# One 4 MB K tile per batch in a cached-attention decode kernel: five shared buffers of 32 KB, all V products by two chunks

## The chip, the cores and the metric

The kernel runs on one core of a Trainium2 chip. The metric is the device time of one execution in microseconds (us). Inputs lie in HBM and are read once.

## The reference

One token for each of eight batches is decoded: layer norm, attention over the last 2048 positions of a cache with 32 query heads that share 8 key heads, an output projection, and a gate from a small MLP.

```python
B, Sq, D = 8, 1, 512
Hq, Hkv, Sk, Dh = 32, 8, 8192, 128
W = min(4096, max(256, Sk // 4))                 # 2048
xn = layernorm(x)
q = (xn @ wq).reshape(B, Sq, Hq, Dh)             # -> b h q d
k = repeat(k_cache[:, :, Sk - W:, :], 4, axis=1) # v alike
p = softmax(einsum("bhqd,bhkd->bhqk", q, k) * Dh ** -0.5)
s = einsum("bhqk,bhkd->bhqd", p, v) -> reshape(B, Sq, Hq * Dh) @ wo
h = sigmoid(xn @ w_gate) * (xn @ w_up)           # D x F, F = 1792
g = silu(h @ w_down)
return x + s * g
```

All tensors are bf16. K and V of the window are 33.6 MB each, wq and wo 4.2 MB each, the three MLP weights 1.8 MB each: 81 MB in all.

## The kernel before

**Loads.** Everything big goes through one ring of nine buffers of 16 KB per partition (2 MB each). A tile of K or V is half a batch: four heads (a "group" gg), 2048 keys; partition p*4+j holds 64 consecutive keys of head j, one run of 16 KB. wq is two tiles, the MLP weights one each, wo two. `loads` lists them by their due times: K tile i at slot 4i, V tile i at slot 4i + 15 (`PV_LAG`), with wg and wu ahead of the last two V tiles, and wd and wo at the end. All are issued by SP, in that order, by `issue_loads()`: load n waits until load n - 9 has been used.

**Slots.** The main loop runs over 64 + 15 slots t, 8 slots per batch; the order in which it writes instructions is the order on each engine. In slot t:

- `k_turn(t)` (L422, DVE): a quarter of K tile t // 4 is transposed in place in 32x32 blocks of 4 byte words, one instruction of 128x1024.
- `qk(t - 4)` (L435, PE): four score matmuls side by side, one for each head of the group, on one of four classes j of the feature index. The moving operand is K with a step of eight elements (16 bytes); it runs over all 512 (chunk, key) columns of the tile. Eight slots fill one PSUM tile `s_ps` for all 32 heads of a batch.
- the softmax of the batch whose scores are complete, spread over phases: maximum `mx` (L447) and `mj` behind the turn in phase 0, `mb` on PE and the exponential on ACT in phase 1, a turn of the probabilities (`pt_bf`, L475) and 16 spreading matmuls (L486) in phase 2, a mask per head on DVE (L506) in phase 3, the denominators (`den_ps`, L528, L530) in phase 4.
- `pv(t - 15)` (L549, PE): a quarter of a V tile against the probabilities. The first six V tiles (`PV_WIDE`) take four chunks of 128 features per matmul (512 columns, weights 64 wide), the others two (256 columns, weights 32 wide). After four slots ACT copies the result, and `pv_sum` (L570, L577) folds the chunks and divides.

So the softmax of batch b - 1 and its V products run among the turns and scores of batch b. The buffers of `mb`, `den_ps`, `oT_ps`, `o2_ps` and `b_ps` are one PSUM bank in turn ("misc").

**The end.** After slot u = 55 of `pv`, `unit_in` multiplies wg and wu (L316), `unit_mid` makes the hidden vector (L330 to L334), `o_rows` (L592, L601) lays the attention output out as rows, `unit_out` multiplies wd (L342), and 64 matmuls with wo (L662) follow as its parts land; `prod` and `y_bf` (L673, L675) and two stores close the kernel.

Of the kernel before, what the change touches and what calls it, by code (L numbers as in the profile page):

```python
# [10 lines left out]
def kernel(  # L11
# [21 lines left out]
    KT = D // P  # L33
# [23 lines left out]
    NA = Dh // 64  # L57
    C4 = 4
    CB = CH // C4
    PV_WIDE = 6  # L60
    RING = 9
    NCOL = 2
    DC = D // NCOL

# [25 lines left out]
            q = nc.sync  # L90
        q.dma_start(out=dst, in_=src)

    def ring_tile(shape, name):
        return ring.tile(shape, bf16, name=name, tag="ring", align_bytes=ALIGN)

    x_bf = work.tile([B, D], bf16, name="x_bf")
    nc.scalar.dma_start(out=x_bf[:], in_=A_x.flatten_outer_dims())

    wq_view = A_wq.rearrange("(p kt) n -> p kt n", kt=KT)
    KH = KT // 2  # L100
    wq_sb = []
    for kh in range(2):
        t = ring_tile([P, KH, Hq * Dh], f"wq_sb{kh}")
        load(t[:], wq_view[:, kh * KH : (kh + 1) * KH, :])
        wq_sb.append(t)

    k_tiles = {}
    v_tiles = {}

    def load_kv(cache, i, name):  # L110
        b, gg = divmod(i, NG)
        t = ring_tile([P, CH, Dh], name)
        load(
            t[:].rearrange("p c d -> p (c d)"),
            cache[b, GL * gg : GL * (gg + 1), win0:Sk, :].rearrange(
                "j (p c) d -> p j (c d)", c=CH
            ),
        )
        return t

    wg_sb = []
    wu_sb = []
    wd_sb = []

    def load_mlp(kind):
        if kind == 2:
            t = ring_tile([P, FT, D], "wd_sb")
            load(t[:], B_w_down.rearrange("(p t) n -> p t n", t=FT))
            wd_sb.append(t)
        else:  # L130
            t = ring_tile([P, KT, F], ("wg_sb", "wu_sb")[kind])
            load(t[:], (B_w_gate, B_w_up)[kind].rearrange("(p kt) n -> p kt n", kt=KT))
            (wg_sb, wu_sb)[kind].append(t)

    loads = [
        (kind, i)
        for _, kind, i in sorted(  # L140
            [(NJ * i, 0, i) for i in range(NT)]
            + [(NJ * i + PV_LAG, 1, i) for i in range(NT)]
        )
    ]
    loads[-2:-2] = [(2, 0), (2, 1)]
    loads = [(4, 0), (4, 1)] + loads + [(2, 2), (3, 0), (3, 1)]
    loads_done = [2]
    released = set()
    wo_view = A_wo.rearrange("(hg p j) n -> p hg j n", p=P, j=4)
    wo_parts = {}  # L150

    def load_wo(half):
        t = ring_tile([P, HG // 2, 4, D], f"wo_sb{half}")
        for h0, h1, j0, j1 in (
            ((0, 2, 0, 4), (2, 4, 0, 4)),
            ((4, 5, 0, 4), (5, 6, 0, 4), (6, 7, 0, 4), (7, 8, 0, 2), (7, 8, 2, 3), (7, 8, 3, 4)),
        )[half]:
            o = half * (HG // 2)
            load(t[:, h0 - o : h1 - o, j0:j1, :], wo_view[:, h0:h1, j0:j1, :])
            for hg in range(h0, h1):  # L160
                for j in range(j0, j1):
                    wo_parts[hg, j] = t[:, hg - o, j, :]

    def issue_loads():
        while loads_done[0] < len(loads):
            n = loads_done[0]
            if n >= RING and loads[n - RING] not in released:
                break
            kind, i = loads[n]
            if kind == 0:  # L170
                k_tiles[i] = load_kv(A_k_cache, i, "k_sb")
            elif kind == 1:
                v_tiles[i] = load_kv(A_v_cache, i, "v_sb")
            elif kind == 2:
                load_mlp(i)
            else:
                load_wo(i)
            loads_done[0] += 1

    issue_loads()  # L180
# [102 lines left out]
    )  # L283

    Sel = {}
    for w in (32, 64):
        Sel[w] = consts.tile([P, w], f32, name=f"Sel{w}")
        nc.vector.tensor_reduce(
            out=Sel[w][:],
            in_=ident[:].rearrange("p (a m) -> p m a", m=w),  # L290
            axis=AX.X,
            op=ALU.add,
        )
# [44 lines left out]
    def unit_out():  # L338
        b_ps = psum1.tile([NCOL * 32, DC], f32, name="b_ps", tag="misc")
        for t in range(FT):  # L340
            for j in range(NCOL):
                nc.tensor.matmul(  # L342
                    b_ps[32 * j : 32 * (j + 1), :],
                    lhsT=hT_sb[:, t, :],
                    rhs=wd_sb[0][:, t, DC * j : DC * (j + 1)],
                    start=(t == 0),
                    stop=(t == FT - 1),
                    tile_position=(0, 32 * j),
                    skip_group_check=True,
                )  # L350
        sigb = work.tile([NCOL * 32, DC], f32, name="sigb")
        nc.scalar.activation(out=sigb[:], in_=b_ps[:], func=AF.Sigmoid)
        nc.vector.tensor_tensor(out=gate[:], in0=sigb[:], in1=b_ps[:], op=ALU.mult)

# [43 lines left out]

    q_tiles = q_projection()
    q_out(0, q_tiles[0], (0, 1))  # L400
    released |= {(4, 0), (4, 1)}
    issue_loads()

    s_tiles = {}
# [8 lines left out]

    def k_turn(t):

        i, j = divmod(t, NJ)
        kw = (
            k_tiles[i][:, CC * j : CC * (j + 1), :]
            .rearrange("p c d -> p (c d)")
            .bitcast(f32)  # L420
        )
        nc.vector.transpose(out=kw, in_=kw)  # L422

    def qk(t):

        i, j = divmod(t, NJ)
        b, gg = divmod(i, NG)
        a, e = divmod(j, 2)
        if gg == 0 and j == 0:
            s_tiles[b] = psum.tile([P, CH * KQ], f32, name="s_ps")  # L430
        kT = k_tiles[i][:].rearrange(
            "p c (a k g e) -> p c a k g e", a=NA, k=KQ, e=2
        )
        for gl in range(GL):
            nc.tensor.matmul(  # L435
                s_tiles[b][32 * gl : 32 * (gl + 1), :],
                lhsT=qz_sb[:, b, GL * gg + gl, j, :],
                rhs=kT[:, :, a, :, gl, e],
                start=(gg == 0 and j == 0),
                stop=(gg == NG - 1 and j == NJ - 1),  # L440
                tile_position=(0, 32 * gl),
                skip_group_check=True,
            )
# [10 lines left out]
    def soft_exp(b, mj):  # L454
        mb_ps = psum1.tile([P, NQ], f32, name="mb_ps", tag="misc")
        nc.tensor.matmul(mb_ps[:], lhsT=SumM[:], rhs=mj[:], start=True, stop=True)  # L456
        nm = small.tile([P, 1], f32, name="nm")
        nc.vector.tensor_reduce(out=nm[:], in_=mb_ps[:], axis=AX.X, op=ALU.min)  # L458
        den128 = small.tile([P, 1], f32, name="den128")
        p_bf = ppool.tile([P, CH * KQ], bf16, name="p_bf")  # L460
        nc.scalar.activation(  # L461
            out=p_bf[:],
            in_=s_tiles.pop(b)[:],
            func=AF.Exp,
            bias=nm[:],
            scale=scale,
            accum_out=den128[:],
        )
        e_tiles[b] = (p_bf, den128)
# [65 lines left out]
    def pv(t):  # L535
# [1 line left out]

        i, j = divmod(t, NJ)
        b, gg = divmod(i, NG)
        n_ch = 4 if i < PV_WIDE else 2  # L540
        w = 16 * n_ch
        if j == 0:
            acc_tiles[i] = psum.tile([P, n_ch * Dh], f32, name="acc_ps")
# [66 lines left out]
    for t in range(NSLOT + PV_LAG):  # L610
# [47 lines left out]
    a_ps = psum.tile([NCOL * 32, DC], f32, name="a_ps", tag="wide")
# [52 lines left out]
```

## Time and profile before

| | |
|---|---|
| time, median of 3 runs (lowest, highest) | 198.31 us (198.0, 199.24) |
| the profiled execution: time, span | 198.21 us, 196.5 us |
| PE busy, DVE busy, ACT busy | 138.2, 117.0, 32.6 us |
| main DMA queue | 81.01 MB, 97.1% of 16 engines' span |
| K turns, L422 | 64 of 1219 ns |
| score matmuls, L435 | 256 of 1065 ns, four at a time |
| V products, L549 | 416 of 345 ns, overlapping |

The span is the time from the first to the last recorded instruction; the execution's own time is 1.71 us longer. Busy times count a stretch once in which instructions overlap, so four matmuls of 1065 ns side by side are about one such stretch. The clock column of the windows is the share of TensorE's full clock that was granted.

### The profile page before, as it was taken

What the parts mean: (1) busy time and instruction counts of PE and PEld (TensorE: products, weight loads), DVE (VectorE), ACT (ScalarE), POOL (GpSimd) and SP (SyncE); (2) the same over time, 40 slices, a digit from 0 to 9 for tenths busy, and PEclk for the clock granted to TensorE, in tenths of its full rate; (3) what the DMA queues carried; (4) which work ended last, traced back from release to release, by engine and by line L of the source; (5) the groups of instructions that cost most, each with busy time, mean ns of one, the idle gap of its engine ahead of it and who ended that gap; (6) DMA issues with size and microseconds to landing.
All of it is one profiled execution on the core that took longest, in us unless ns stands there. A gap on an engine that the chain in (4) does not pass through costs nothing.

```text
span 196.5 us, 2699 instructions
## 1 busy us (share of the span) xinstructions
PE 138.2 (70%) x1112; PEld 57.6 (29%) x1112; DVE 117.0 (60%) x200; ACT 32.6 (17%) x68; POOL 9.3 (5%) x21
## 2 busy tenths in 40 slices
PE   0340078669998987899789278946794779674783
PEld 0110011032324222423333044404240424443661
DVE  3818999746686828664777277837773750361101
ACT  3008540410121102101210021002100210340000
POOL 8820000000000000000000000000000000000000
PEclk9999999955999997879999957996888587996579
DMA  6999999999999999999999999999999999999991
GB/s 215 429 427 427 430 434 429 440 434 427 434 427 434 427 427 427 430 434 430 430 434 434 424 427 440 430 425 427 430 434 430 427 431 434 423 424 420 411 391 41
DMA packets 6860, 81.19 MB, mean 413 GB/s; under 512 B 792, under 2 KB 1088, under 8 KB 2112
## 3 DMA queue, kind: packets, MB, share of 16 engines
q1 hardware_dynamic: 6752, 81.01, 97.1%
q8 instruction: 8, 0.13, 0.2%
q10 hardware_dynamic: 32, 0.01, 0.1%
q14 instruction: 4, 0.03, 0.0%
q0 software_dynamic: 64, 0.01, 0.0%
HBM read 81.02 MB, written 0.01 MB: 412 GB/s over the span
## 4 chain that ended last, share of the span: by engine, by line
DMA 72%; DVE 17%; PE 8%; ACT 1%; issue 1%; SPq 0%; DVEq 0%; ACTq 0%
DMA k_sb<-in_A_k_cache_dram 47%; DMA wd_sb<-in_B_w_down_dram 14%; DVE k_sb L422 11%; DMA wq_sb<-in_A_wq_dram 6%; DMA wo_sb<-in_A_wo_dram 5%; PE pT_ps L486 3%; PE s_ps L435 3%; DVE qz_sb L395 2%; PE acc_ps L549 1%; DVE mx L447 1%; DVE qT_sb L386 1%; DVE pt_bf L475 1%; ACT L461 1%; PE q_ps L367 1%; PE mb_ps L456 0%
## 5 line engine op out<-in xcount | busy, mean ns | idle before, releaser
L422 DVE STREAM_TRANSPOSE k_sb<-k_sb 128x1024 f32<-128x1024 f32 x64 | 75.9, 1219 | 16.6 <-DMA k_sb<-in_A_k_cache_dram 16.5
L435 PE MATMUL s_ps<-k_sb,qz_sb 128*32 128x512 bf16 x256 | 68.7, 1065 | 16.4 <-DVE k_sb L422 11.6
L549 PE MATMUL acc_ps<-v_sb,pT_sb 128*32 128x256 bf16 (+1 forms) x416 | 35.3, 345 | 3.9 <-DMA v_sb<-in_A_v_cache_dram 2.6
L549 PEld LDWEIGHTS <-pT_sb 128*32 128x32 bf16 (+1 forms) x416 | 12.5, 109 | 33.2 <-issue 27.0
L506 DVE TENSOR_SCALAR pT_sb<-pc_bf,Hm 128x512 bf16<-128x512 bf16 x32 | 9.1, 349 | 18.3 <-ACT pc_bf L495 18.3
L435 PEld LDWEIGHTS <-qz_sb 128*32 128x32 bf16 x256 | 8.3, 100 | 34.0 <-issue 26.1
L560 ACT COPY acc_sb<-acc_ps 128x256 f32<-128x256 f32 (+1 forms) x16 | 7.2, 453 | 63.2 <-PE acc_ps L549 63.2
L486 PE MATMUL pT_ps<-pt_bf,spread 128*128 128x128 bf16 x128 | 12.5, 272 | 6.3 <-DVE pt_bf L475 6.3
L570 PEld LDWEIGHTS oT_ps<-Sel,acc_sb 128*128 128x128 f32 x88 | 11.8, 202 | 14.3 <-ACT acc_sb L560 8.5
L570 PE MATMUL oT_ps<-Sel,acc_sb 128*128 128x16 f32 x88 | 13.4, 276 | 1.1 <-ACT acc_sb L560 1.1
L486 PEld LDWEIGHTS <-spread 128*128 128x128 bf16 x128 | 10.8, 123 | 10.8 <-DVE pt_bf L475 10.8
L456 PE MATMUL mb_ps<-mj,SumM 128*128 128x4 f32 x16 | 3.5, 286 | 14.3 <-DVE mj L449 14.3
L461 ACT ACTIVATE p_bf<-s_ps,nm 128x512 bf16<-128x512 f32 x8 | 5.5, 687 | 46.5 <-DVE nm L458 46.5
L577 DVE TENSOR_TENSOR oT_sb<-oT_ps,rden 128x16 bf16<-128x16 f32 x16 | 2.6, 160 | 11.7 <-PE oT_ps L570 11.7
L456 PEld LDWEIGHTS mb_ps<-mj,SumM 128*128 128x128 f32 x16 | 2.8, 218 | 22.5 <-DVE mj L449 20.6
L397 ACT COPY qz_sb<-qT_sb 32x128 bf16<-32x128 bf16 x20 | 8.3, 413 | 3.0 <-DVE qT_sb L386 2.7
L530 DVE RECIPROCAL rden<-den_ps 128x32 f32<-128x32 f32 x8 | 2.8, 351 | 7.3 <-PE den_ps L528 7.3
L495 ACT CAST pc_bf<-pT_ps 128x512 bf16<-128x512 f32 x8 | 4.7, 587 | 13.1 <-PE pT_ps L486 13.1
L367 PE MATMUL q_ps<-wq_sb,xnT_sb 128*32 128x512 bf16 x32 | 3.8, 625 | 4.0 <-DMA wq_sb<-in_A_wq_dram 4.0
L475 DVE STREAM_TRANSPOSE pt_bf<-p_bf 128x512 bf16<-128x512 bf16 x8 | 5.4, 679 | 1.9 <-ACT p_bf L461 1.9
L662 PE MATMUL a_ps<-wo_sb,o_sb 128*32 128x256 bf16 x64 | 5.5, 315 | 1.0 <-DMA wo_sb<-in_A_wo_dram 0.9
L447 DVE TENSOR_REDUCE mx<-s_ps 128x1 f32<-128x512 f32 x8 | 5.3, 657 | 0.0
(61 smaller groups left out, 61.9 us busy)
## 6 DMA issues: line engine op xcount, KB each, us to landing
k_sb<-in_A_k_cache_dram SPq DMA_DIRECT2D x16, 2048.0 KB, 31.8
v_sb<-in_A_v_cache_dram SPq DMA_DIRECT2D x16, 2048.0 KB, 29.5
wq_sb<-in_A_wq_dram SPq DMA_DIRECT2D x2, 2048.0 KB, 9.7
wo_sb<-in_A_wo_dram SPq DMA_DIRECT2D x2, 1024.0 KB
wg_sb<-in_B_w_gate_dram SPq DMA_DIRECT2D x1, 1792.0 KB, 29.3
wu_sb<-in_B_w_up_dram SPq DMA_DIRECT2D x1, 1792.0 KB, 30.1
wd_sb<-in_B_w_down_dram SPq DMA_DIRECT2D x1, 1792.0 KB, 27.6
wo_sb<-in_A_wo_dram SPq DMA_DIRECT2D x3, 512.0 KB, 23.5
```

Of the source, the lines that this page charges most:

```text
L397: nc.scalar.copy(out=out, in_=in_)
L422: nc.vector.transpose(out=kw, in_=kw)
L435: nc.tensor.matmul(s_tiles[b][32 * gl : 32 * (gl + 1), :], lhsT=qz_sb[:, b, GL * gg + gl, j, :], rhs=kT[:, :, a, :, gl, e], start=(gg == 0 ...
L447: nc.vector.reduce_max(out=mx[:], in_=s_tiles[b][:], axis=AX.X)
L456: nc.tensor.matmul(mb_ps[:], lhsT=SumM[:], rhs=mj[:], start=True, stop=True)
L461: nc.scalar.activation(out=p_bf[:], in_=s_tiles.pop(b)[:], func=AF.Exp, bias=nm[:], scale=scale, accum_out=den128[:],)
L475: nc.vector.transpose(out=pt_bf[:].rearrange("p c g q r -> p (c g q r)"), in_=p_bf[:])
L486: nc.tensor.matmul(pT_ps[:, :, c4, :], lhsT=spread[:, c4, Q, :], rhs=pt[:, :, Q, :], start=(Q == 0), stop=(Q == NQ - 1), skip_group_check= ...
L506: nc.vector.tensor_scalar(out=pT_tiles[b][:, :, gl, :], in0=pc, scalar1=Hm[:, gl : gl + 1], scalar2=None, op0=ALU.mult,)
L549: nc.tensor.matmul(acc_tiles[i][w * c : w * (c + 1), :], lhsT=pT[:, 32 * y : 32 * y + w], rhs=v_tiles[i][:, ch : ch + n_ch, :].rearrange(" ...
L560: nc.scalar.copy(out=acc_sb[:], in_=acc_tiles.pop(i)[:])
L570: nc.tensor.matmul(oT_ps[:], lhsT=acc_sb[:, Dh * c : Dh * (c + 1)], rhs=sel[:, c // 2, c % 2], start=(c == 0), stop=(c == n_ch - 1),)
```

## The change

K comes as one tile of 4 MB for each batch: all eight heads, partition p*8+h holds 128 consecutive keys of head h, one run of 32 KB. Each buffer of the ring is 32 KB per partition, and there are five. V of a batch is one buffer too, filled by two loads of 2 MB as before; wq is one buffer with two loads, wg and wu share one, wd and wo have one each. The order of the loads is written out: wq, K0, then K(i+1) and V(i) in turn, V7, wg and wu, wd, wo. So the MLP's input weights now come behind the last V.

The turns of a batch (eight instructions of the same size) are written in the first four of its eight slots, two in each. A score matmul takes one head's feature class over all 128 chunks of the tile, with a step of sixteen elements (32 bytes). The four heads of a matmul group are half of the tile's heads, and the first slot's group already reads the whole length of every partition. The exponential writes its output in the old order of keys. K of a batch is released at the end of slot 11 counted from its own first, V at the end of its eight slots.

All V products take two chunks. `unit_in` for wg is written after slot u = 59 and for wu after u = 63, and `unit_mid` follows there.

```diff
-    PV_WIDE = 6
-    RING = 9
+    RING = 5
+    PK = P // Hkv
+    CK = W // PK
+    KK = PK // NQ
+    HS = CK // CH
+    KS = 2
+    CT = CK // (SPB)
...
-    def ring_tile(shape, name):
-        return ring.tile(shape, bf16, name=name, tag="ring", align_bytes=ALIGN)
+    def ring_tile(name):
+        return ring.tile([P, UNIT], bf16, name=name, tag="ring", align_bytes=ALIGN)
...
+    def load_k(b):
+        t = ring_tile("k_sb")
+        load(
+            t[:],
+            A_k_cache[b, :, win0:Sk, :].rearrange("h (p c) d -> p h (c d)", c=CK),
+        )
+        k_tiles[b] = t[:].rearrange("p (c d) -> p c d", d=Dh)
+
+    def load_v(b):
+        t = ring_tile("v_sb")
+        for gg in range(NG):
+            h = t[:, HALF * gg : HALF * (gg + 1)]
+            load(
+                h,
+                A_v_cache[b, GL * gg : GL * (gg + 1), win0:Sk, :].rearrange(
+                    "j (p c) d -> p j (c d)", c=CH
+                ),
+            )
+            v_tiles[NG * b + gg] = h.rearrange("p (c d) -> p c d", d=Dh)
...
+    loads = [(5, 0), (0, 0)]
+    for i in range(B - 1):
+        loads += [(0, i + 1), (1, i)]
+    loads += [(1, B - 1), (2, 0), (3, 0), (4, 0)]
+    loads_done = [0]
...
     def k_turn(t):
 
-        i, j = divmod(t, NJ)
-        kw = (
-            k_tiles[i][:, CC * j : CC * (j + 1), :]
-            .rearrange("p c d -> p (c d)")
-            .bitcast(f32)
-        )
-        nc.vector.transpose(out=kw, in_=kw)
+        b, j = divmod(t, SPB)
+        for n in range(KS * j, min(KS * (j + 1), SPB)):
+            kw = (
+                k_tiles[b][:, CT * n : CT * (n + 1), :]
+                .rearrange("p c d -> p (c d)")
+                .bitcast(f32)
+            )
+            nc.vector.transpose(out=kw, in_=kw)
 
     def qk(t):
 
-        i, j = divmod(t, NJ)
-        b, gg = divmod(i, NG)
-        a, e = divmod(j, 2)
...
+        b, j = divmod(t, SPB)
+        y, gg = divmod(j, NG)
+        a, e = divmod(y, 2)
+        if j == 0:
+            s_tiles[b] = psum.tile([P, CK * KK], f32, name="s_ps")
+        kT = k_tiles[b].rearrange("p c (a k g e) -> p c a k g e", a=NA, k=KK, e=2)
         for gl in range(GL):
             nc.tensor.matmul(
                 s_tiles[b][32 * gl : 32 * (gl + 1), :],
-                lhsT=qz_sb[:, b, GL * gg + gl, j, :],
-                rhs=kT[:, :, a, :, gl, e],
-                start=(gg == 0 and j == 0),
-                stop=(gg == NG - 1 and j == NJ - 1),
+                lhsT=qz_sb[:, b, GL * gg + gl, y, :],
+                rhs=kT[:, :, a, :, GL * gg + gl, e],
+                start=(j == 0),
+                stop=(j == SPB - 1),
...
         nc.scalar.activation(
-            out=p_bf[:],
-            in_=s_tiles.pop(b)[:],
+            out=p_bf[:].rearrange("p (c k h) -> p h c k", k=KK, h=HS),
+            in_=s_tiles.pop(b)[:].rearrange("p (h c k) -> p h c k", k=KK, h=HS),
...
-        n_ch = 4 if i < PV_WIDE else 2
+        n_ch = 2
...
-        if t % NJ == NJ - 1 and QK_LAG <= t < NSLOT + QK_LAG:
-            released.add((0, t // NJ - 1))
-        if u >= 0 and u % NJ == NJ - 1:
-            released.add((1, u // NJ))
-        issue_loads()
-        if u == NSLOT - 2 * NJ - 1:
+        if t % SPB == QK_LAG - 1 and SPB <= t < NSLOT + QK_LAG:
+            released.add((0, t // SPB - 1))
+        if u >= 0 and u % SPB == SPB - 1:
+            released.add((1, u // SPB))
+        if u == NSLOT - NJ - 1:
             unit_in(wg_sb[0])
-            unit_in(wu_sb[0])
-            released |= {(2, 0), (2, 1)}
-            issue_loads()
-        if u == NSLOT - 2 * NJ:
-            unit_mid()
         if u == NSLOT - NJ:
             o_rows(0)
+        if u == NSLOT - 1:
+            unit_in(wu_sb[0])
+            released.add((2, 0))
+            unit_mid()
+        issue_loads()
     pv_sum(NT - 1)
     o_rows(1)
     unit_out()
```

More of the change, by code (lines that the diff above doesn't have):

```diff
@@ L52 @@
     NSLOT = B * SPB
+    UNIT = 2 * CH * Dh
     QK_LAG = NJ
@@ L100 @@
     KH = KT // 2
+    HALF = UNIT // 2
     wq_sb = []
[L102 to L105, printed above, removed]
     k_tiles = {}
     v_tiles = {}
-    def load_kv(cache, i, name):
-        b, gg = divmod(i, NG)
[L112 to L117, printed above, removed]
-        )
-        return t
     wg_sb = []
@@ L123 @@
     wd_sb = []
[L125 to L148, printed above, removed]
     wo_view = A_wo.rearrange("(hg p j) n -> p hg j n", p=P, j=4)
     wo_parts = {}
-    def load_wo(half):
-        t = ring_tile([P, HG // 2, 4, D], f"wo_sb{half}")
-        for h0, h1, j0, j1 in (
[L155 to L159, printed above, removed]
+    def load_wq(i):
+        t = ring_tile("wq_sb")
+        for kh in range(2):
+            h = t[:, HALF * kh : HALF * (kh + 1)].rearrange("p (kt n) -> p kt n", kt=KH)
+            load(h, wq_view[:, kh * KH : (kh + 1) * KH, :])
+            wq_sb.append(h)
@@ new lines, in load_in, with load_down @@
+    def load_in(i):
+        t = ring_tile("wgu_sb")
+        for n, (w, to) in enumerate(((B_w_gate, wg_sb), (B_w_up, wu_sb))):
+            h = t[:, KT * F * n : KT * F * (n + 1)].rearrange("p (kt n) -> p kt n", kt=KT)
+            load(h, w.rearrange("(p kt) n -> p kt n", kt=KT))
+            to.append(h)
+    def load_down(i):
+        t = ring_tile("wd_sb")
+        h = t[:, : FT * D].rearrange("p (t n) -> p t n", t=FT)
+        load(h, B_w_down.rearrange("(p t) n -> p t n", t=FT))
+        wd_sb.append(h)
@@ L160, in load_wo @@
+    def load_wo(i):
+        t = ring_tile("wo_sb")[:].rearrange("p (hg j n) -> p hg j n", hg=HG, j=4)
+        for h0, h1, j0, j1 in (
+            (0, 2, 0, 4),
+            (2, 4, 0, 4),
+            (4, 5, 0, 4),
+            (5, 6, 0, 4),
+            (6, 7, 0, 4),
+            (7, 8, 0, 2),
+            (7, 8, 2, 3),
+            (7, 8, 3, 4),
+        ):
+            load(t[:, h0:h1, j0:j1, :], wo_view[:, h0:h1, j0:j1, :])
             for hg in range(h0, h1):
                 for j in range(j0, j1):
-                    wo_parts[hg, j] = t[:, hg - o, j, :]
+                    wo_parts[hg, j] = t[:, hg, j, :]
@@ L164, in issue_loads @@
+    loaders = (load_k, load_v, load_in, load_down, load_wo, load_wq)
+    loads = [(5, 0), (0, 0)]
[3 more added lines that the diff above has]
+    loads_done = [0]
+    released = set()
     def issue_loads():
@@ L169, in issue_loads @@
             kind, i = loads[n]
[L170 to L177, printed above, removed]
+            loaders[kind](i)
             loads_done[0] += 1
@@ L285 @@
     Sel = {}
-    for w in (32, 64):
+    for w in (32,):
         Sel[w] = consts.tile([P, w], f32, name=f"Sel{w}")
@@ L350, in unit_out @@
                 )
-        sigb = work.tile([NCOL * 32, DC], f32, name="sigb")
+        sigb = ppool.tile([NCOL * 32, DC], f32, name="sigb", tag="p_bf")
         nc.scalar.activation(out=sigb[:], in_=b_ps[:], func=AF.Sigmoid)
@@ L400 @@
     q_out(0, q_tiles[0], (0, 1))
-    released |= {(4, 0), (4, 1)}
+    released.add((5, 0))
     issue_loads()
@@ L414, in k_turn @@
     def k_turn(t):
-        i, j = divmod(t, NJ)
-        kw = (
-            k_tiles[i][:, CC * j : CC * (j + 1), :]
-            .rearrange("p c d -> p (c d)")
-            .bitcast(f32)
-        )
-        nc.vector.transpose(out=kw, in_=kw)
-    def qk(t):
-        i, j = divmod(t, NJ)
-        b, gg = divmod(i, NG)
-        a, e = divmod(j, 2)
[L429 to L433, printed above, removed]
+        b, j = divmod(t, SPB)
[6 more added lines that the diff above has]
+            nc.vector.transpose(out=kw, in_=kw)
+    def qk(t):
+        b, j = divmod(t, SPB)
[4 more added lines that the diff above has]
+        kT = k_tiles[b].rearrange("p c (a k g e) -> p c a k g e", a=NA, k=KK, e=2)
         for gl in range(GL):
@@ L564, in pv_sum @@
         b, gg = divmod(i, NG)
-        n_ch = 4 if i < PV_WIDE else 2
+        n_ch = 2
         acc_sb = acc_sbs.pop(i)
@@ L653 @@
     unit_out()
-    released.add((2, 2))
-    issue_loads()
     a_ps = psum.tile([NCOL * 32, DC], f32, name="a_ps", tag="wide")
```

## The prediction

> **What bounds the kernel now.** I read the page's busy shares and DMA rows first, then the chain that ended last, then the order of time from 150 us on.
>
> ```profile
> DMA  6999999999999999999999999999999999999991
> ...
> q1 hardware_dynamic: 6752, 81.01, 97.1%
> ```
>
> One queue moves 81 MB and keeps the 16 DMA engines busy for 97.1% of the span of 196.5 us; PE has 70%, DVE 60%. No transfer pauses between the first slice and the last. The kernel is bound by its loads, and the compute engines only have to keep up and to finish soon after the last byte. The last steps of the chain that ended last (start, length, what) say the same:
>
> ```profile
> 183.06 9.89 DMA wo_sb<-in_A_wo_dram
> 192.95 0.04 issue
> 192.99 0.30 PE a_ps L662 x2
> ```
>
> The last piece of wo lands at 192.95; behind it stand two matmuls, two DVE operations and the store. So a change can help only by moving bytes faster, and hurts if the stream gets a hole or if compute is not done with everything else by 193. How near is compute to that? The order of time at the end (start, length, engine, line; the bracket is idle time and its releaser):
>
> ```profile
> 150.77 1.25 DVE L422 STREAM_TRANSPOSE k_sb<-k_sb 128x1024 f32<-128x1024 f32 x1 [3.31 <-DMA k_sb<-in_A_k_cache_dram]
> ...
> 172.06 1.14 DVE L506 TENSOR_SCALAR pT_sb<-pc_bf,Hm 128x512 bf16<-128x512 bf16 x4 [1.82 <-ACT pc_bf L495]
> ...
> 178.80 0.62 PE L549 MATMUL acc_ps<-v_sb,pT_sb 128*32 128x256 bf16 x8 [2.09 <-DMA v_sb<-in_A_v_cache_dram]
> ...
> 186.81 3.32 PE L662 MATMUL a_ps<-wo_sb,o_sb 128*32 128x256 bf16 x40
> ...
> 190.45 0.61 PE L662 MATMUL a_ps<-wo_sb,o_sb 128*32 128x256 bf16 x8 [0.32 <-DMA wo_sb<-in_A_wo_dram]
> ```
>
> The last K tile (2 MB) lands at 150.77, its last score matmul ends at 166.42, the last softmax's mask at 173.20. From there PE waits for V (2.09 us), and at 190.45 for wo. Compute reaches the wo matmuls at 186.81 and catches up with the stream at about 190: some 3 us to spare, no more. That margin decides this change.
>
> **Bytes and runs.** The same 81 MB move. Only the price of a packet changes. In the windows from 184 to 189, where 4 KB runs of wo arrive, the rate is 418, 418, 418, 426 and 418 GB/s; with 16 KB runs it is about 429. Per engine that is 0.1562 us for 4 KB and 0.6110 us for 16 KB, hence about 0.0046 us per packet and 1.2174 us for 32 KB instead of 1.2220. K is 33.6 MB, 78 us of stream: 0.3 us gained. An estimate; no row has 32 KB runs, so I keep 0 and 2 us (429 to 434 GB/s) as its ends.
>
> **The ring.** Five buffers of 4 MB instead of nine of 2 MB; each is freed only when the whole tile is used. A tile is overwritten by the load five places later, whose transfer starts four transfers (4 x 9.83 us) after this tile's stream has ended, some 37 us after it landed (landing follows the stream by about 2 us). K is freed after 8 turns (9.8 us, below) and 8 score groups (12.4 to 15.5 us): 22 to 26 us. V of the batch before lands 9.8 us after K of this batch, and its last product comes some 5 us after the next K is turned: 19.7 + 9.8 + 5 - 9.8 = 25 us. Both leave more than 10 us, so I price the coarser ring at nothing. SP issues in order, but releases come in the order of the loads.
>
> **V by two chunks.** For the first six of the sixteen V tiles, 16 wide matmuls become 32 narrow ones, 96 more in all. A slot of 8 narrow ones takes 0.24 us at full clock (145.35 to 145.59), of 4 wide ones 0.4 to 0.55; the six sums fall from 8 passes (1.07 us) to 4 (0.62). PE gains a few us in the first three batches, where the stream covers it: nothing.
>
> **Turns and scores: the part that costs.** K of the last batch still stands behind 60 MB of loads, so its last half lands when the last K tile lands now, 150.77 less 0.3: 150.5. But nothing of these 4 MB can be turned before that. Now DVE has four turns left there; then it has eight, and a score matmul reads all 128 key chunks, so it waits for all eight. The softmax of batch 6 (mx, L447) stands behind the eight turns on DVE, PE's products of batch 6 behind that softmax. Step by step:
>
> - Turns: 8 x 1.145 (3.43 us for three) + 0.1, the reciprocal 0.33 and an output product 0.17 between them: 9.8. At 160.3 PE may start.
> - Scores: 8 groups of four x 0.887 (start to start from 25.06 to 27.72) = 7.1. Between them on PE 7 slots of V products 1.7, mb 0.4, spread 1.03, a sum 0.55, den 0.5, and about 1.1 of waiting for batch 6's exp, turn, cast and mask: 12.4 at full clock. At half clock the V products take 0.43, spread 1.89, a sum 1.04: 15.5. Half of each: 13.9, to 174.2.
> - Softmax 7: 6.8 now (166.42 to 173.20), 0.8 more with a slow spread; 7.2, to 181.4. The exponential's new output order (elements 4 bytes apart) is taken at nothing: ACT's cast that permutes its input (L381) takes 0.59 us as the one that doesn't (L495). At worst its 0.69 doubles.
> - Products of batch 7: all eight slots stand behind this softmax, as they did; but V, at 169 to 170 now, has landed before it, and both input matmul groups of the MLP stand among them (wg before the last four slots, wu behind them; both were done at 173.0 before). 8 x 0.24, den 0.5, 2 x 0.77, sum and rows with their waits 0.95: 4.9. At half clock 8.9; I take 7.9, to 189.3.
> - Sigmoid 0.54, product 0.62, turn 1.00, output product 0.17, rows 0.36, cast 0.73, hand-overs: 3.7, to 193.0. These had stood in V's wait before; that cover is gone.
> - b_ps: 28 x 0.105 = 2.94 as now. wo has landed, so 64 matmuls run through: 15 at 0.105 and 49 at 0.053: 4.2. To 200.1.
> - prod, y and the store as now: 0.85 + 2.46.
>
> Span 203.4. The profiled execution took 198.21 with a span of 196.5, and 1.71 lies around it: **205.1**. The median of the runs shown is 198.31, so it stands for them.
>
> Why half clock: the windows (length, PE busy, clock, DMA share, GB/s) show it behind every idle stretch.
>
> ```profile
> 150.00:151.00 1.00, 0.00 (x0) 1.00 1.03 442
> 151.00:152.00 1.00, 0.00 (x0) 0.61 1.05 442
> ...
> 163.00:164.00 1.00, 1.00 (x12) 0.50 1.04 444
> ...
> 187.00:188.00 1.00, 1.00 (x14) 0.50 1.04 426
> 188.00:189.00 1.00, 1.00 (x16) 0.61 1.02 418
> ```
>
> 3.3 us of idleness at 149.6 cost half the clock until 158; it fell again from 161.7 to 165 behind a gap of 0.9 us with PE busy most of the time, and stayed low from 178.7 to 188.5 behind waits of 2 us and less. The changed kernel leaves PE idle for some 6 us during the turns, then has gaps of 0.5 to 1.5 us in softmax 7, then 3.7 us before b_ps. With the full clock throughout, the sum is 150.5 + 9.8 + 12.4 + 6.8 + 4.9 + 3.5 + 4.9 + 3.3 = 196.1, which the landing of wo holds at about 196.3: 198.0 in all. With the half clock in every part (b_ps and wo as above): 208.4.
>
> [...]
>
> **Rivals.**
> 1. The clock holds: from 160 on PE stays at full clock and everything but wo is done by 193; the load stream sets the end as now. 198.0, the side that is not slower; it decides as soon as the sum falls below the last landing. For it: 165 to 178.7 ran at full clock. Against: three of the last five waits brought it down. 0.14.
> 2. Score matmuls read at twice the stride (32 bytes instead of 16, heads now eight deep). At 16 bytes four of them take 0.887 us, where four contiguous ones took 0.43 at 13 us (L367); so stride already costs. Nearest row with a 32 byte step: the spread, 512 steps in 1.03 us, 2.0 ns each against 0.43 now, but each step there carries four elements. [...] At twice the price: 7.1 us more behind the last K, 212.2, and PE's 19.3 us per batch fill the 19.7 us period, so it drifts up to 10 us more: 215. 0.13. [...]
> 3. The ring stalls: releases come over 10 us later than worked out, and each us beyond costs one per batch; 2 us over six batches, 217. The wait of SP would stand on V's products, as 89.9 us of its waits do now without harm. 0.04.
> 4. The long runs gain more than 1% of the stream and the clock holds: 196. 0.03. This is also the only case in which the change pays as a bigger transfer.
>
> **How the numbers follow.** Forecast 0.66, at 205.1, from 199 to 209.5. About 1% (2 us) is what a measurement tells from no change. Faster is rival 4: 0.03. Same is rival 1 and the low tail of the forecast: 0.17. Slower is the rest: 0.80. Only the forecast's own range would leave out too much; carried down to 198.0 it takes in rival 1, and carried up to 210.0 a clock that is low in every part. Rivals 2, 3 and 4, 0.20 together, stay outside.
>
> **What would show it.** Right: the last k_sb lands at 150 to 151 with eight turns behind it; the first score group of batch 7 at 160, the last near 174; b_ps at 191 to 194; the wo matmuls in one run without waiting for DMA; the chain's end on PE and DVE, not on wo. The stream should show no hole before 190. Wrong: a score group of well over 1.1 us, wo matmuls waiting for their transfer, or SP issuing a tile after the transfer ahead of it has ended.

## Result and profile after

The changed kernel takes 295.97 us in the median of six runs (291.49 to 313.27), the kernel before 198.31. The forecast was 205.1, its range 198.0 to 210.0. The loss is some 98 us where 7 were expected. The ratio, 1.478 (95% interval 1.469 to 1.487), is that of the three fastest executions (median 293.33 us) and leaves out the slowest, 313.27 us, which was the profiled one, so the rows below are those of a second profiled execution, of 294.06 us (span 292.3; called e7 below).

The rate on the page of before, and then the rows of e7's page that answer to those of before:

```profile
GB/s 215 429 427 427 430 434 429 440 434 427 434 427 434 427 427 427 430 434 430 430 434 434 424 427 440 430 425 427 430 434 430 427 431 434 423 424 420 411 391 41
...
DMA  7999999999999998999999989999999999999930
GB/s 289 399 202 206 211 211 206 382 332 215 213 323 390 202 213 260 404 215 213 231 446 224 213 195 401 278 215 206 342 352 197 213 278 427 430 422 423 415 115 1
...
q1 hardware_dynamic: 5600, 81.01, 95.4%
```

This is the lesson of the case. The engines are nearly as busy as before (95.4% against 97.1%), with the same 81.01 MB, but "busy" is the time that packets are open, not what they carry: the rate falls from about 430 GB/s to 202 to 215 in long stretches. By windows (length, PE, PEld, DVE, ACT and POOL busy, clock, DMA share, GB/s):

```profile
104.00:113.00 9.00, 3.16 (x28) 0.56 (x20) 0.00 (x0) 0.38 (x1) 0.00 (x0) 0.95 0.96 202
...
117.00:126.00 9.00, 2.94 (x28) 1.66 (x28) 8.45 (x11) 0.00 (x0) 0.00 (x0) 0.50 1.13 379
...
250.00:262.00 12.00, 11.37 (x112) 4.15 (x111) 3.38 (x11) 1.85 (x4) 0.00 (x0) 0.91 1.00 429
```

A K tile is under way in the first, V mostly in the second, V and the MLP's weights in the third. The page's groups say who pays (behind the first bar busy time and mean of one in ns, behind the second the idle time before them); first the turns of before, then turns and scores of e7:

```profile
L422 DVE STREAM_TRANSPOSE k_sb<-k_sb 128x1024 f32<-128x1024 f32 x64 | 75.9, 1219 | 16.6 <-DMA k_sb<-in_A_k_cache_dram 16.5
...
L434 DVE STREAM_TRANSPOSE k_sb<-k_sb 128x1024 f32<-128x1024 f32 x64 | 73.5, 1206 | 104.3 <-DMA k_sb<-in_A_k_cache_dram 104.3
L445 PE MATMUL s_ps<-k_sb,qz_sb 128*32 128x512 bf16 x256 | 70.6, 1117 | 69.6 <-DVE k_sb L434 69.6
```

DVE waits 104.3 us for K (16.5 before), PE 69.6 us for the turns behind it (11.6 before). No instruction became dear: a turn takes 1206 ns (1219), a score matmul 1117 (1065). The chain that ended last:

```profile
191.31 49.20 DMA k_sb<-in_A_k_cache_dram
240.54 2.37 DVE k_sb L434 x2
...
249.94 1.15 PE s_ps L445 x4
...
281.84 3.17 PE b_ps L353 x28
285.01 4.18 PE a_ps L669 x64
```

The last K tile lands at 240.54; the forecast said 150.5. What follows it takes 292.3 - 240.54 = 51.8 us; the forecast said 203.4 - 150.5 = 52.9. So the whole error lies ahead of the last K landing: in how fast K comes.

### The profile page after: what moved, and what is told of

It is laid out like the page before. It is cut to its first block, busy times and chain, and to the rows that moved or that the text cites. A ratio compares the mean times of both kernels' runs of the same rounds, so it can differ in the third digit from the quotient of the medians.

```text
span 311.5 us, 2825 instructions
## 1 busy us (share of the span) xinstructions
PE 128.8 (41%) x1184; PEld 55.5 (18%) x1184; DVE 116.3 (37%) x199; ACT 32.1 (10%) x68; POOL 9.1 (3%) x21
## 3 DMA queue, kind: packets, MB, share of 16 engines
q1 hardware_dynamic: 5600, 81.01, 91.6%
## 4 chain that ended last, share of the span: by engine, by line
another core or an unknown queue 26%; DMA 26%; DVE 25%; PE 16%; ACT 3%; issue 2%; SPq 0%; ACTq 0%
DMA k_sb<-in_A_k_cache_dram 26%; DVE k_sb L434 19%; PE s_ps L445 6%; PE acc_ps L559 3%; PE pT_ps L496 2%; DVE pT_sb L516 2%; ACT p_bf L471 1%; PE a_ps L669 1%; DVE pt_bf L485 1%; ACT pc_bf L505 1%; PE mb_ps L466 1%; PE b_ps L353 1%; PE d_ps L327 1%; PE oT_ps L580 1%
## 5 line engine op out<-in xcount | busy, mean ns | idle before, releaser
L434 DVE STREAM_TRANSPOSE k_sb<-k_sb 128x1024 f32<-128x1024 f32 x64 | 73.5, 1207 | 124.4 <-DMA k_sb<-in_A_k_cache_dram 124.4
L445 PE MATMUL s_ps<-k_sb,qz_sb 128*32 128x512 bf16 x256 | 70.5, 1114 | 70.2 <-DVE k_sb L434 70.2
L559 PE MATMUL acc_ps<-v_sb,pT_sb 128*32 128x256 bf16 x512 | 30.3, 331 | 3.4 <-DVE pT_sb L516 3.4
L580 PEld LDWEIGHTS oT_ps<-Sel,acc_sb 128*128 128x128 f32 x64 | 11.9, 263 | 100.8 <-issue 94.1
L445 PEld LDWEIGHTS <-qz_sb 128*32 128x32 bf16 x256 | 8.3, 107 | 81.4 <-issue 59.9
L471 ACT ACTIVATE p_bf<-s_ps,nm 128x512 bf16<-128x512 f32 x8 | 7.0, 875 | 150.4 <-DVE nm L468 150.4
L559 PEld LDWEIGHTS <-pT_sb 128*32 128x32 bf16 x512 | 13.2, 110 | 32.8 <-issue 26.6
L496 PE MATMUL pT_ps<-pt_bf,spread 128*128 128x128 bf16 x128 | 9.6, 231 | 5.6 <-DVE pt_bf L485 5.6
L570 ACT COPY acc_sb<-acc_ps 128x256 f32<-128x256 f32 x16 | 6.0, 373 | 51.2 <-PE acc_ps L559 51.2
L496 PEld LDWEIGHTS <-spread 128*128 128x128 bf16 x128 | 8.1, 102 | 8.9 <-DVE pt_bf L485 8.9
L468 DVE TENSOR_REDUCE nm<-mb_ps 128x1 f32<-128x4 f32 x8 | 1.3, 162 | 14.7 <-PE mb_ps L466 14.7
L669 PE MATMUL a_ps<-wo_sb,o_sb 128*32 128x256 bf16 x64 | 4.1, 290 | 0.0
## 6 DMA issues: line engine op xcount, KB each, us to landing
v_sb<-in_A_v_cache_dram SPq DMA_DIRECT2D x16, 2048.0 KB, 51.8
wd_sb<-in_B_w_down_dram SPq DMA_DIRECT2D x1, 1792.0 KB, 19.2
```

Of the source, the lines that this page charges most:

```text
L445: nc.tensor.matmul(s_tiles[b][32 * gl : 32 * (gl + 1), :], lhsT=qz_sb[:, b, GL * gg + gl, y, :], rhs=kT[:, :, a, :, GL * gg + gl, e], star ...
L471: nc.scalar.activation(out=p_bf[:].rearrange("p (c k h) -> p h c k", k=KK, h=HS), in_=s_tiles.pop(b)[:].rearrange("p (h c k) -> p h c k", ...
L496: nc.tensor.matmul(pT_ps[:, :, c4, :], lhsT=spread[:, c4, Q, :], rhs=pt[:, :, Q, :], start=(Q == 0), stop=(Q == NQ - 1), skip_group_check= ...
L559: nc.tensor.matmul(acc_tiles[i][w * c : w * (c + 1), :], lhsT=pT[:, 32 * y : 32 * y + w], rhs=v_tiles[i][:, ch : ch + n_ch, :].rearrange(" ...
L580: nc.tensor.matmul(oT_ps[:], lhsT=acc_sb[:, Dh * c : Dh * (c + 1)], rhs=sel[:, c // 2, c % 2], start=(c == 0), stop=(c == n_ch - 1),)
L669: nc.tensor.matmul(a_ps[32 * c : 32 * (c + 1), :], lhsT=o2_sb[:, hg, j, :], rhs=wo_parts[hg, j][:, DC * c : DC * (c + 1)], start=(n == 0), ...
```

## Experiments

**Which property of the load is slow? (p1)** Loads alone, three tiles of 4 MB of each kind.

```diff
+ for pattern in patterns:        # each three times, five buffers of 4 MB, all issued by SP
+     dma_start(out=t[:, c0:c0+w], in_=src)
+     tensor_copy(out=mark, in_=t[:, c0:c0+1])     # its start marks the landing (L91)
...
```

> Loads only, no computation of the reference: 13 patterns of reading the K cache, three tiles of 4 MB each, into five buffers; a one-column copy on VectorE marks each landing. In order: V's pattern (two loads of 4 heads x 32 partitions x 16 KB); the changed K pattern (8 heads, pitch 2 MB, 16 x 32 KB); the same with the heads' pitch made 2 MB + 4 KB; the changed pattern in two loads of 16 KB runs; one contiguous 4 MB piece in 32 KB runs; eight contiguous 512 KB pieces; 4 heads x 32 partitions x 32 KB; 8 heads x 16 partitions x 16 KB; 2 heads x 64 x 32 KB; pitch 2 MB + 16 KB; 8 heads with 24 KB runs; pitch 2 MB + 32 KB; V's pattern again. Theory A (eight heads 2 MB apart collide in HBM): about 205 GB/s for the changed pattern, for its 16 KB loads and for 8 heads x 16 KB; 420 or more with the odd pitch, contiguous, and with 4 heads. Theory B (runs of 32 KB are slow from wherever): about 205 for every pattern with 32 KB runs, 420 or more for all with 16 KB runs. Theory C (neither alone, but which partitions are written together when heads are innermost and eight deep): 205 for every pattern with eight pieces, the odd pitches and the 512 KB pieces among them.

The order of time on DVE, one line for each landing (start, length; the bracket is the wait): the end of V, the first two changed K tiles, then a tile in contiguous 32 KB runs.

```profile
33.20 0.16 DVE L91 COPY mark<-t 128x1 bf16<-128x1 bf16 x1 [5.17 <-DMA t<-in_A_k_cache_dram]
53.27 0.16 DVE L91 COPY mark<-t 128x1 bf16<-128x1 bf16 x1 [19.91 <-DMA t<-in_A_k_cache_dram]
73.30 0.16 DVE L91 COPY mark<-t 128x1 bf16<-128x1 bf16 x1 [19.88 <-DMA t<-in_A_k_cache_dram]
...
221.84 0.16 DVE L91 COPY mark<-t 128x1 bf16<-128x1 bf16 x1 [9.48 <-DMA t<-in_A_k_cache_dram]
231.49 0.16 DVE L91 COPY mark<-t 128x1 bf16<-128x1 bf16 x1 [9.49 <-DMA t<-in_A_k_cache_dram]
```

| source of one 128-partition load | us per 4 MB |
|---|---|
| V: 32 pieces x 4 heads, 16 KB | 2 x 4.85 |
| changed K: 16 pieces x 8 heads, 32 KB | 20.05 |
| the same with the heads 4 to 32 KB further apart | 20.0 |
| the same in contiguous memory | 20.0 |
| 16 x 8, 16 KB runs, two loads | 2 x 9.8 |
| 16 x 8, 24 KB runs (3 MB) | 14.9 for 3 MB |
| 32 x 4, 32 KB | 9.7 to 11.4 |
| 64 x 2, 32 KB | 9.64 |
| 128 contiguous runs of 32 KB | 9.64 |

Whatever is sixteen pieces by eight is slow, by a factor of two and at any run length, pitch or place in memory that was tried: theory C. 32 KB runs as such go at 435 GB/s. Why two of the three 32 x 4 tiles of 32 KB took 11.2 and 11.4 us is open.

**K fetched like V, in the changed kernel (e1).**

```diff
-        load(t[:], A_k_cache[b, :, win0:Sk, :].rearrange("h (p c) d -> p h (c d)", c=CK))
+        for gg in range(NG):
+            load(t[:, HALF * gg : HALF * (gg + 1)],
+                 A_k_cache[b, GL * gg : GL * (gg + 1), win0:Sk, :].rearrange("j (p c) d -> p j (c d)", c=CH))
```

> The changed kernel, but each K tile is loaded by two loads of 4 heads x 32 partitions x 16 KB, as V is; the rest is unchanged, so the scores belong to keys and heads in another order than the reference's. If the slow K loads are the whole loss, the stream is whole again: 198 by the theory that nothing else in the change costs, 205 (199 to 209) by the prediction's sum for the longer tail of turns, scores and softmax behind the last K.

200.69 us, 1.0118 times before (1.0102 to 1.0135): 95 of the 98 us are back, with the five buffers, the wide stride and the late MLP all in place. The loss is the load's shape. The wait for eight turns is softened here, as half a tile lands earlier: the last batch's turns begin at 145.78, in e3 below at 150.38.

**The same 16 x 8 split with 16 KB runs, in the changed kernel (e2).**

```diff
+        v = A_k_cache[b, :, win0:Sk, :].rearrange("h (p c) d -> p h c d", c=CK)
+        for g in range(HS):
+            load(t[:, HALF * g : HALF * (g + 1)], v[:, :, CH * g : CH * (g + 1), :].rearrange("p h c d -> p h (c d)"))
...
```

> The changed kernel with each K tile in two loads of 16 KB runs (the lower and the upper 64 keys of each partition), eight heads in both, result as the reference's. Theory B (long runs): 198 to 209. Theory A and C (eight heads): as the changed kernel, 290 to 313.

289.67 us (285.72 and 293.62), about as slow as the changed kernel: neither the run length nor the size of the load is the cause.

**Where the bytes are written (p2).** Loads alone again, 2 MB into 64 partitions, once 0 to 63, once 32 to 95, from the same source.

```diff
+ t[p0 : p0 + 64] <- K[b, 0:4, win0:Sk, :].rearrange("h (p c) d -> p h (c d)", c=128)   # p0 = 0, then 32
+ t[p0 : p0 + 64] <- 64 contiguous runs of 32 KB                                          # p0 = 0, then 32
...
```

> Loads only, no computation of the reference. Nine groups: the changed K pattern (three tiles); the same tile as 16 KB runs, lower half on SP's queue and upper half on ACT's (three); one 1 MB load alone on ACT's queue that puts four steps ahead of the next group on that queue; the two-queue tiles again, now with ACT's half four heads out of step (three); 16 key blocks x 4 heads x 32 KB into partitions 0 to 63, 2 MB each (four); the same into partitions 32 to 95 (four); 2 MB of contiguous rows into partitions 0 to 63 (four) and into 32 to 95 (four); the changed pattern (two). [...] Theory E (a source of 16 x 8 pieces is slow by its own descriptors, the destination is indifferent): 20 us per tile on two queues in either phase, and no difference between 0 to 63 and 32 to 95.

Landings (L78), two into 0 to 63 and then two into 32 to 95:

```profile
193.68 0.15 DVE L78 COPY mark<-t 64x1 bf16<-64x1 bf16 x1 [10.11 <-DMA t<-in_A_k_cache_dram]
203.92 0.15 DVE L78 COPY mark<-t 64x1 bf16<-64x1 bf16 x1 [10.08 <-DMA t<-in_A_k_cache_dram]
...
223.23 0.15 DVE L78 COPY mark<-t 32x1 bf16<-32x1 bf16 x1 [4.68 <-DMA t<-in_A_k_cache_dram]
228.06 0.15 DVE L78 COPY mark<-t 32x1 bf16<-32x1 bf16 x1 [4.68 <-DMA t<-in_A_k_cache_dram]
```

10.2 us against 4.83 for the same bytes; contiguous runs do the same (10.2 and 4.84). So the partitions that are written decide, and theory E, by which they make no difference, falls. The 4.83 hold while only loads into 32 to 95 are under way: the last load of that group took 9.85 us (228.06 to 237.91), and the last two of the contiguous one 6.08 and 10.67, with the next group's loads behind them on the same queue. The second queue ran ahead of its tiles, so the groups with two queues, and the tiles ahead of them, tell nothing.

**The forecast's own case: everything of the change but the slow load (e3).** K comes as one 4 MB load in 64 x 2 pieces, so from two heads.

```diff
-            A_k_cache[b, :, win0:Sk, :].rearrange("h (p c) d -> p h (c d)", c=CK),
+            A_k_cache[b, 0:2, :, :].rearrange("h (p c) d -> p h (c d)", c=CK),
```

> The changed kernel with each K tile still one 4 MB load with one landing and 32 KB runs, but read from two heads' whole caches (64 blocks of 2 heads, a pattern that took 9.64 us per 4 MB in the loads-only run), so it attends other keys than the reference. The scores can't begin before the whole tile is turned. By the prediction's sum 205 (199 to 209); if the tail costs no more than in the kernel with K loaded like V, 200.7.

204.71 us in the median of five (202.95, 205.06, 204.71, 205.04, 200.26), ratio 1.034 (1.0323 to 1.0358). The profiled execution is the one of 202.95 (span 201.2). Its chain:

```profile
172.02 0.93 PE s_ps L445 x3
...
179.20 1.15 DVE pT_sb L516 x4
...
186.66 1.28 ACT L341
187.95 0.55 ACT sig L341
...
191.48 3.08 PE b_ps L353 x28
194.56 3.51 PE a_ps L669 x64
```

**The other way round: the kernel before with its K tiles split 16 x 8 (e4).**

```diff
...
+            else cache[b, :, win0 + W // 2 * gg : win0 + W // 2 * (gg + 1), :].rearrange("h (p c) d -> p h (c d)", c=CH)
```

> The kernel before, all its tiles, order and compute unchanged, except that a K tile of 2 MB is 8 heads x 16 blocks x 16 KB instead of 4 x 32, so the scores belong to other heads and keys. If the load pattern alone is the loss, 16 tiles at 9.8 instead of 4.9 us each: 198 + 78 = 277. If the big tile or the five buffers are needed for the loss: about 198.

328.77 us (325.79 and 331.75). The split alone does it, with nine small buffers and nothing else of the change. But it costs 52 us more than the 277 that the loads alone had said, and V's share of the stream is slow too: by the trace's packet records (start, length and size of every DMA packet) 77% of the 16 KB packets from 12 us on take over 1 us, where K has half of them; before, 0.2% do. The page's rate:

```profile
GB/s 300 338 223 223 213 214 336 219 322 211 288 203 258 201 238 203 217 228 223 219 223 225 213 230 219 203 221 227 209 217 228 205 217 274 368 432 422 415 197 31
```

**The rest of e1: is it the MLP's place? (e5)** e1 with wg and wu ahead of the last V again, and their products behind slot u = 55, four and eight slots earlier.

```diff
-    loads += [(1, B - 1), (2, 0), (3, 0), (4, 0)]
+    loads += [(2, 0), (1, B - 1), (3, 0), (4, 0)]
...
-        if u == NSLOT - NJ - 1:
+        if u == NSLOT - 2 * NJ - 1:
             unit_in(wg_sb[0])
...
```

> The changed kernel with K loaded like V (which took 200.69) and, beside that, wg and wu loaded ahead of the last V and their matmuls and the hidden vector put back to slots u = 55 and 56, as in the kernel before; scores in another order than the reference's, as there. If the 2.4 us that are left over the kernel before stand in the MLP's late place (the sum's two groups of 16 matmuls and its step of 3.7 us for the sigmoid, product and turn), b_ps starts some 4 us earlier, wo's landing ends the kernel again, and it takes 198.3. If they stand in the scores' wait for eight turns, 200 or more.

199.43 us, ratio 1.0049 (1.0031 to 1.0067): 1.3 of e1's 2.4 us are the MLP's late place.

**Two queues for K (e6).** Lower half of the tile by SP, upper half by ACT.

```diff
+            load(t[:, HALF * g : HALF * (g + 1)], v[:, :, CH * g : CH * (g + 1), :].rearrange("p h c d -> p h (c d)"), queues[g])
```

> The changed kernel with each K tile in two loads of 16 KB runs, eight heads in both, the lower half issued by SP and the upper half by ACT; result as the reference's. The same two loads from SP alone took 289.67. [...] Theory E (the source pattern is slow by its own descriptors): 285 or more.

315.76 us, where the author's estimate for queues at different heads was 200 to 250: a miss. Theory E's 285 or more holds here, but p2's 10.2 against 4.83 us speak against it. Both queues write the same partitions; why two are no faster than one, no run shows.

**The changed kernel once more (e7)**, for its profile (shown above): 294.06 us.

> The changed kernel as it is, for a second profile. By loads alone: K 33.6 MB at 209 GB/s and 47.5 MB at 429 are 160 + 111 us, with 3 us before and some 16 behind the last landing 290; any more must be V's loads held up by K's.

**Do K and V disturb each other, and does a shift help? (p3)** Loads alone: K and V in turn, then K halves on two queues, also behind fillers that shift one queue.

```diff
+ groups = [[p_k, p_v] * 4, [p_k2, p_v2] * 8, [p_two] * 4, [p_fill] + [p_two] * 4, [p_fill8] + [p_two] * 4]
```

> Loads only, no computation of the reference; the queues run empty before each group. Group 1: four tiles of the changed K pattern (4 MB) and four of V's pattern (4 MB) in turn; group 2: eight loads of 8 heads x 16 x 16 KB (2 MB) and eight of V's pattern (2 MB) in turn; group 3: four K tiles in 16 KB runs, lower half on SP, upper on ACT, both from their first head; group 4: the same behind a load of four steps per engine on ACT's queue; group 5: the same behind a load of eight steps, after which both queues are at the same head again. Alone, K's pattern takes 20.0 us and V's 9.7 us per 4 MB. If K and V don't disturb each other, 29.7 us per pair in group 1 and 14.7 in group 2; the changed kernel shows 31.1, the kernel before with 8 heads some 18. [...] Theory E (the source pattern itself): no difference between 3, 4 and 5.

The K tiles of K and V in turn land at 24.14, 53.94, 83.77 and 113.65, so a pair takes 29.84 us, just the sum of both alone. In 2 MB tiles a pair takes 14.8 to 15.4 us, near the sum of 14.7; in e4, where such tiles alternate too, K tiles land 20.2, 19.5, 19.3 and 20.2 us apart (105.93 to 185.07), so the loads alone do not repeat what made e4 so slow. The halves on two queues take 18 to 20 us a tile with and without fillers (the last tile of a group less); the author's estimate of about 10 behind a filler was missed. Both fillers are cut into sixteen pieces, as the K tile is, and such a load keeps all sixteen engines busy (a DMA share of 1.00 at 210 GB/s from 40 to 50, under a K tile alone). So the fillers held up no engine more than another, and did not test whether engines disturb each other.

**Engines against each other (p4).** Loads that use only some engines, and one that holds up four of them (in short form).

```diff
+ two(m):          t[0 : 2m]      <- K[b, 0:2, 0 : 64 * m, :]    "h (s c) d -> h s (c d)", c=64      # groups 1 to 3
+ blocks(n, m, p0): t[p0 : p0+nm] <- K[b, 0:m, win0 : win0 + 128 * n, :] "h (o c) d -> o h (c d)", c=128
+ groups = [two(16)]*2, [two(64)]*2, [two(32)]*2, [blocks(4,8)]*2, [blocks(8,4)]*2, [blocks(8,8)]*3,
+          [blocks(4,4,64)] + [blocks(8,8)]*4,  [blocks(4,4,64)] + [p_k, p_v]*4
```

> Loads alone, eight groups, each begun when the one before has landed; nothing of the reference is computed. [...] Rival R: the shape of the split sets an engine's rate, 27 GB/s with four rows per outer index, half with eight. A 16 KB run takes 0.611 us, 32 KB 1.213. [...]

The DMA share in windows of groups 2, 4 and 6 (length, DVE and POOL busy, clock, DMA share, GB/s), 0.12, 0.25 and 0.53 of sixteen engines, is that of two, four and about eight: as many as the source has outer pieces.

```profile
70.00:100.00 30.00, 0.00 (x0) 0.00 (x0) 1.00 0.12 54
...
182.00:188.00 6.00, 0.00 (x0) 0.00 (x0) 1.00 0.25 109
...
230.00:240.00 10.00, 0.00 (x0) 0.00 (x0) 1.00 0.53 115
```

Landings (L85): the second load of group 4, the second of group 6, the first two of group 7, and in group 8 two K tiles and the last half of the V tile between them.

```profile
188.94 0.14 DVE L85 COPY mark<-t 32x1 bf16<-32x1 bf16 x1 [9.39 <-DMA t<-in_A_k_cache_dram]
...
244.04 0.15 DVE L85 COPY mark<-t 64x1 bf16<-64x1 bf16 x1 [19.21 <-DMA t<-in_A_k_cache_dram]
...
283.83 0.15 DVE L85 COPY mark<-t 64x1 bf16<-64x1 bf16 x1 [11.85 <-DMA t<-in_A_k_cache_dram]
...
295.74 0.15 DVE L85 COPY mark<-t 64x1 bf16<-64x1 bf16 x1 [11.70 <-DMA t<-in_A_k_cache_dram]
...
355.57 0.16 DVE L85 COPY mark<-t 128x1 bf16<-128x1 bf16 x1 [19.83 <-DMA t<-in_A_k_cache_dram]
...
369.79 0.16 DVE L85 COPY mark<-t 128x1 bf16<-128x1 bf16 x1 [9.44 <-DMA t<-in_A_k_cache_dram]
...
389.65 0.16 DVE L85 COPY mark<-t 128x1 bf16<-128x1 bf16 x1 [19.64 <-DMA t<-in_A_k_cache_dram]
```

Groups 1, 2, 4, 5 and 6 take 9.6, 38.8, 9.6, 4.8 and 19.3 us a load. What the rows of one engine cost one after the other is an estimate from 0.611 us for 16 KB and 1.213 for 32 KB: 16, 64, eight and four rows make 9.8, 39.1, 9.7 and 4.85 us, as groups 1, 2, 4 and 5 have it; group 6, eight rows on each of eight engines, takes twice its 9.7. Rival R wanted 19.4 for group 4. Eight rows per engine are not slow in themselves: four engines with eight rows each, into partitions 0 to 31, carry 109 GB/s, eight engines with eight rows each, into 0 to 63, 115. Group 7 is the strongest evidence: the very loads of group 6 take 11.9 us instead of 19.3 once four of the engines are held up by a load of four rows ahead of them. By R they would still take 19.4; with no hindrance left, 9.7. In the packet records the four held-up engines begin the load at 271.24 to 271.30, and the others begin their fourth row by 271.37, so they are three rows apart and not four. Whether that is why 11.9 and not 9.7 is not shown.

Group 3, two pieces of 32 rows into partitions 0 to 31 and 32 to 63, lies between 19.6 and 39.1, 32 rows at 0.611 us and twice that. Its first load took 37.4 us (142.30 - 104.89), some 34 without the 3.4 us more that the first load of group 2 took than its second; its second took 23.8 (166.12 - 142.30). So two engines that write there hinder each other, where the two of group 2, into 0 to 63 and 64 to 127, do not (38.8 for 64 rows). Why the second load lost so much less than the first, no run shows. Group 8: 34.3, 34.4, 35.3 and 29.3 us a pair, 33.3 on the mean, against 29.84 with all engines in step: now the second V half of the first three pairs takes 9.7 to 10.0 us where beside K in p3 it took 5.1.

**V by two chunks alone, in the kernel before (e8).**

```diff
-    PV_WIDE = 6
+    PV_WIDE = 0
```

> The kernel before, with one edit of the change alone: all V products by two chunks. The prediction prices it at nothing, as the first three batches are covered by the stream: 198.3, within 0.5 us. Rival: the extra 96 matmuls delay the early buffers and the stream shows a hole: 199 to 201.

199.31 us, ratio 1.0037 (1.0019 to 1.0054): about 0.7 us, not nothing. Near the end PE waits for wo; behind that landing stand sixteen matmuls where two stood before:

```profile
192.88 1.54 PE L662 MATMUL a_ps<-wo_sb,o_sb 128*32 128x256 bf16 x16 [0.60 <-DMA wo_sb<-in_A_wo_dram]
```

So it is the stream's tail that is later, not PE: by the packet records the last 4 KB packet of wo ends at 192.47, before at 191.32. Why is not settled. A candidate is a 16 KB packet of the queue that the page calls "instruction": here it stands at 187.47, late among the wo packets, before at 182.48, early among them.

## Why the prediction was wrong, and where it was right

**What happens.** Sixteen engines work through a load side by side, and of the loads of p4 each keeps as many of them busy as its source has outer pieces (0.12, 0.25 and 0.53 of sixteen for two, four and eight). In the changed K tile there are sixteen pieces, and partition 8p + h takes piece p of head h. What a load then costs depends on which partitions are written together: 2 MB take 10.2 us into 0 to 63 and 4.83 into 32 to 95 (p2); eight rows per engine take 9.6 us on four engines and 19.3 on eight, and 11.9 on the same eight once four are held up (p4). So engines at work at the same moment hinder each other by where they write, and sixteen pieces of eight partitions run at half the rate: 20.05 us for 4 MB, 209 GB/s. V, 32 pieces of four partitions, runs at 432. Which engine takes which partition no view shows, nor by what the engines hinder each other; that the K tile loses its half as the eight engines of p4 lose theirs is inferred from p2 and p4. The two-queue loads (e6 with 315.76 us, and p3 with 18 to 20 us a tile behind its fillers) came out slower than the author's estimates, 200 to 250 and about 10, and no run says why.

**The step that failed: "Bytes and runs".** It took 9.8 us for a K tile and 0 to 2 us of gain for the whole of K as the ends. Measured: 20.05 us a tile. The step asked what a packet of 32 KB costs and never which partitions the packets go to, though the diff replaced four heads by eight in the one expression that decides it. Its packet price was right for the shape it had in mind (9.64 us per 4 MB, 1.213 us a packet in the trace's packet records, 1.2174 forecast); in the K tile of that same trace a packet takes 2.36 to 2.57 us. No row of before has such a load, so the end of this unknown should have been drawn at half the rate, not at 2 us.

**The size.** The last K landed 90.2 us later than in e3 (240.54 - 150.38). Eight tiles at 20.05 instead of 9.64 make 83. For the other 7: from the second tile to the last, K lands 30.8 to 31.9 us apart where loads alone took 29.84. In the packet records of e7 the first and the last engine to begin a K tile are 0.5 us apart at the first tile and 1.0, 1.7, 2.2, 2.6, 3.2, 3.8 and 4.6 us later on, 0.3 to 0.4 in p3. Engines out of step also make a pair of K and V longer: 33.3 us in group 8 of p4, 29.84 in p3.

The same drift goes with the changed kernel's spread. In the execution of 313.27 us one engine begins the last K tile 18.9 us behind the first and ends it at 257.96; in e7, of 294.06 us, the last packet of K ends at 239.40. These 18.6 us are nearly all of the 19.2 between the two. That the drift also made e4 so slow fits, but is only argued.

What first pulls the engines apart is open. The packet records show a candidate: packets of the queue called "instruction", each in the way of one engine. In e7 one of 8 KB stands at 57.77, and the next K tile finds one engine 1.2 us behind the others; in that tile one of 16 KB takes 1.38 us (76.56), and so in every K tile from there on. The loads-only runs have no such packet of 16 KB. No run takes them out of the changed kernel.

**What held.** e3 has every other term of the sum in place. Its steps fell near the forecast ones; that its median came within 0.4 us of 205.1 is in part luck, as the profiled execution was some 2 us and the fastest 4.8 us below the forecast:

| | forecast | e3 |
|---|---|---|
| last K lands | 150.5 | 150.38 |
| first score group | 160.3 | 159.79 |
| scores end | 174.2 | 172.95 |
| mask ends | 181.4 | 180.35 |
| V products and MLP input done, the sigmoid's step begins | 189.3 | 186.66 |
| b_ps begins | 193.0 | 191.48 |
| wo matmuls end | 200.1 | 198.07 |
| time | 205.1 | 202.95; median 204.71 |

- The ring: no stall; the last K landed to 0.1 us as forecast. Rival 3 falls. (The landing, taken about 2 us behind the stream, came 1.25 us behind the last packet of K in before, 149.52 to 150.77, and 1.1 in e7, 239.40 to 240.54.)
- Turns and scores: the one wait for eight turns costs what was worked out. Rival 2, twice the price at a 32 byte step, falls: in e3 score groups follow each other, with a slot of V products between them, every 1.16 us (170.69 to 171.85), and L445 has 1119 ns where L435 had 1065. No row of before shows the sum's 0.887 us for a group at a step of 32 bytes; the 1.16 us of e3 stand against 1.17 at 16 bytes in before, also with a slot of V products between (144.42 to 145.59). The exponential's new order, taken at nothing, costs 0.83 us in place of 0.69.
- The products took 6.3 us where 7.9 were taken. The hand-over to b_ps took 4.8 where 3.7 were taken: ACT loads its table for the sigmoid there (1.28 us, shown above; in before the ACT_TABLE_LOAD at 172.04, also 1.28), which the sum left out.
- The clock: in e3 it was 0.72 during the turns, 0.50 from 160 to 163, 1.00 from 164 to 172, 0.66 on the mean from 176 to 186 (its record has 0.50 from 177.3 to 184.1 and 1.00 on both sides), 0.50 at b_ps, 0.96 under wo. So the half clock came in the parts that the prediction named, though not through all of wo, and rival 1, in which it holds, was not seen: the fastest of e3's five runs took 200.26. The half clock from 177.3 on stands behind idle stretches of PE of at most 1.4 us.
- V by two chunks: forecast nothing, measured 0.7 us. The MLP's late place, part of the products' 7.9 us, is worth 1.3 (e1 against e5).
- Rival 4, long runs that gain over 1%: 435 GB/s in place of 432 for loads alone, 0.7%; the reason is real, the size too small to matter, and the split undid it.
- The sum for a half clock in every part, 208.4, adds up from the prediction's own terms to 208.2; nothing hangs on it.

## What to carry to other kernels

Read the GB/s row beside the DMA row: engines that hinder each other are busy (95.4% here, at 202 to 215 GB/s in long stretches). When an edit changes how a load's source is cut, ask which partitions are written at the same time. For 128 partitions, sixteen pieces of eight took 20.05 us per 4 MB here, and 32, 64 and 128 pieces, of at most four partitions each, 9.64 to 9.7, but for two tiles of 32 with 11.2 and 11.4. Stay with a cut that has been measured, or measure the load alone, which takes one run. A bound for an operation that no row shows must be drawn from what could go wrong with it, not only from the nearest price.

## What was not expected of the hardware

- A load that covers all 128 partitions can run at 209 GB/s instead of 432, by how its source is split alone.
- 2 MB into partitions 0 to 63 take 10.2 us, into 32 to 95 4.83.
- Out of step can help or harm: four engines held up made eight-engine loads faster (19.3 to 11.9 us), and made V slower beside the changed K (5.1 to about 9.8 us for its second half).
- DMA packets of the instruction queue stand in the same engines' way: in e7 one of 16 KB took 1.38 us in the middle of a K tile, and one engine's K packets pause from 76.58 to 77.92.
